# Attention in steps of four heads on the array's quarters, with MLP units in the last eight steps

## The chip, the cores and the metric

One core of a Trainium2 chip runs the kernel. The metric is the device time in microseconds of one execution; of the kernel before there are three runs. Times inside the kernel come from one profiled execution of it.

## The reference

```python
def _attn_ref(q, k, v, cap):            # (4, 12, 448, 64) each
    scale = 1.0 / np.sqrt(q.shape[-1])
    scores = scale * np.matmul(q, k.transpose(0, 1, 3, 2))
    scores = cap * np.tanh(scores / cap)
    scores = scores - np.max(scores, axis=-1, keepdims=True)
    attn = np.exp(scores)
    attn = attn / (np.sum(attn, axis=-1, keepdims=True) + 1e-09)
    return np.matmul(attn, v).astype(np.float32)

def _moe_ref(x, w1, w2, w3, w_out):     # x (1792, 768), weights (768, 768)
    h = np.maximum(np.maximum(x @ w1, x @ w2), x @ w3)
    return (h @ w_out).astype(np.float32)
...
    x = np.ascontiguousarray(attn_out.transpose(0, 2, 1, 3)).reshape(B * S, H * D)
    return _moe_ref(x=x, **moe_kwargs)
```

The cap is 30, so the kernel takes its branch without the row maximum (the tanh bounds the scores; the maximum cancels but for the 1e-9, which is scaled instead).

## The kernel before

**Attention.** There are 24 pairs of heads, one step each. The 448 keys of a pair are three tiles of 128 for each head and a tail tile that holds the last 64 keys of both heads. `scores` (L127) multiplies the three tiles, the two heads on the upper and lower 64 rows of the array, into three double banks `qk`; `scores_tail` (L136) multiplies the tail on the whole array with a block-diagonal key tile `kb`. ScalarE turns each tile into tanh (`tanh`, L145) and later into exp (`expo`, L149) in the tile `e_t`. `values_tail` and `values` (L152, L159) multiply with the values, the two heads on the left and right 64 columns of the array, and `sums` (L179) multiplies the VectorE sum `s_t` of the exp tiles with ones. `normalize` (L186) takes the reciprocals between two 32x32 transposes and multiplies; `split_x` (L197) writes the result as two fp32r tiles, `xh` and what that leaves, `xl`. All of these products are f32 and show in the trace as two matmul records each.

**MLP.** 24 weight tiles (18 for w1, w2, w3, then 6 for w_out) meet 4 batches of 448 tokens: 96 units (`unit`, L258). A unit is 18 fp32r matmuls (6 chunks of 128 inputs, three of the four high and low products each) into one bank. ScalarE copies the first of three weights into `m`, VectorE takes the maximum with the others. When the 18th weight tile of a batch is done, `split_h` (L278) splits that batch's six tiles for the last layer, a ScalarE cast and a VectorE subtraction each. The weights come as float64 words and `conv` (L233) makes two fp32r tiles of each in four steps: a ScalarE piece (L241) and a VectorE piece, two more VectorE pieces (L246, L250), then the ScalarE cast with L253 and a VectorE subtraction.

**Order.** The order on every engine is written out by hand in `rest` (L284); each engine works through its own list and waits where an operand is not there. In a step the products of pair i come first (scores), then values and sums of pair i-1, then its normalization; ScalarE does the tanh of pair i and, after those, its exp. The conversion of the first two weight tiles lies in the last eight steps. Only the first two units of the MLP stand ahead of the last pair's values. Loads go through SP's queue, two steps ahead.

Of the kernel before, what the change touches and what calls it, by code (L numbers as in the profile page):

```python
# [28 lines left out]
AHEAD = 2  # L29
UNITS_AHEAD = 2  # L30

EARLY = NP - 8
# [3 lines left out]
def attn_max_mlp_kernel(ctx: ExitStack, tc: tile.TileContext, q, k, v, kt, vt, cap, wts, out):  # L36

# [31 lines left out]
    q_t = ring("q_t", 3, [128, S])  # L69
    k_t = ring("k_t", 3, [128, NT * 128])  # L70
    v_t = ring("v_t", 3, [128, NT, 2, D])
    kb = ring("kb", 2, [128, PB, 128])
    vb = ring("vb", 2, [128, PB, 128])
    e_t = ring("e_t", 2, [128, 2 * NT + 1, S])
    s_t = ring("s_t", 2, [128, 2, S])
    tt_t, rb_t, xf_t = (ring(n, 2, [128, S]) for n in ("tt_t", "rb_t", "xf_t"))
    r_t = ring("r_t", 2, [128, QB])
    xh = ring("xh", NP, [128, S], F32R)
    xl = ring("xl", NP, [128, S], F32R)
# [4 lines left out]
    wl = ring("wl", 3, [128, KC, 128], F32R)  # L84

    qk = ring("qk", 3, [128, 2, 512], pool=psum)
    bk = ring("bk", 2, [128, 512], pool=psum)


    spare = [t[:, i, :] for t in e_t for i in range(2 * NT + 1)]  # L90
    spare += [t[:, i, :] for t in s_t for i in range(2)] + [*tt_t, *rb_t, *xf_t]
    m_t = {(b, f): m_0[b] if f == 0 else spare[B * (f - 1) + b] for f in range(KC) for b in range(B)}
    o_t = [*q_t, *spare[B * (KC - 1):]]

    banks = [t[:, i, :] for i in range(2) for t in qk] + [*bk]
# [4 lines left out]
    def flat(t):  # L100
        return t.rearrange("p a b -> p (a b)")


    def load_batch(b):
        for src, dst in ((kt, kb[b % 2]), (vt, vb[b % 2])):
            for h in range(2):
                r = slice(64 * h, 64 * h + 64)
                nc.sync.dma_start(out=dst[r, :, r], in_=src[b][r])

    def load(p):  # L110
        nc.sync.dma_start(out=k_t[p % 3], in_=k[p])
        nc.sync.dma_start(out=q_t[p % 3], in_=q[p])
        if p == 0:
            load_batch(0)
        nc.sync.dma_start(out=v_t[p % 3], in_=v[p])
        if p % PB == PB - 2 and p + 2 < NP:
            load_batch(p // PB + 1)

    turn = [0]

    def bank():
        turn[0] += 1
        return bk[turn[0] % 2]

    ps_tail, ps_av = {}, {}

    def scores(p):  # L127
        kt_, qt_ = k_t[p % 3], q_t[p % 3]
        for j in range(NT):
            for h in range(2):  # L130
                r = slice(64 * h, 64 * h + 64)
# [4 lines left out]
    def scores_tail(p):  # L136
        ps_tail[p] = bank()
        nc.tensor.matmul(ps_tail[p][:, 0:S], kb[p // PB % 2][:, p % PB, :], q_t[p % 3], start=True, stop=True)  # L138

    def e_of(p, j):  # L140

        e = e_t[p % 2]
        return e[:, 2 * NT, :] if j == NT else e[:, 2 * j:2 * j + 2, :]

    def tanh(p, j):  # L145
        src = ps_tail[p][:, 0:S] if j == NT else qk[j][:, :, 0:S]
        nc.scalar.activation(out=e_of(p, j), in_=src, func=AF.Tanh, scale=sc_t)  # L147

    def expo(p, j):  # L149
        nc.scalar.activation(out=e_of(p, j), in_=e_of(p, j), func=AF.Exp, scale=acap)  # L150

    def values_tail(p):  # L152
        ps_av[p] = bank()
        nc.tensor.matmul(  # L154
            ps_av[p][:, 0:S], vb[p // PB % 2][:, p % PB, :], e_of(p, NT), start=True, stop=False,
            skip_group_check=True,
        )

    def values(p):  # L159
        for j in range(NT):  # L160
            for h in range(2):
                nc.tensor.matmul(  # L162
                    ps_av[p][64 * h:64 * h + 64, 0:S], v_t[p % 3][:, j, h, :], e_of(p, j)[:, h, :],
                    start=False, stop=(j == NT - 1), skip_group_check=True,
                )

    def add_two(p):
        tt(nc.vector, flat(s_t[p % 2]), flat(e_of(p, 0)), flat(e_of(p, 1)), ALU.add)

    def add_rest(p):  # L170
        s = s_t[p % 2]
        for h in range(2):
            r = slice(64 * h, 64 * h + 64)
            tt(nc.vector, s[r, h, :], s[r, h, :], e_of(p, NT)[r], ALU.add)
        tt(nc.vector, flat(s), flat(s), flat(e_of(p, 2)), ALU.add)

    ps_sum = {}

    def sums(p):  # L179
        ps_sum[p] = bank()  # L180
        for h in range(2):
            nc.tensor.matmul(  # L182
                ps_sum[p][64 * h:64 * h + 64, 0:S], ones, s_t[p % 2][:, h, :], start=True, stop=True
            )

    def normalize(p, eps):  # L186

        t, r, rb, xf = tt_t[p % 2], r_t[p % 2], rb_t[p % 2], xf_t[p % 2]
        nc.vector.transpose(out=t, in_=ps_sum[p][:, 0:S])  # L189
        nc.vector.tensor_scalar_add(r, t.rearrange("p (a b) -> p a b", b=32)[:, :, 0], eps)  # L190
        nc.vector.reciprocal(r, r)
        nc.vector.transpose(  # L192
            out=rb.rearrange("p (a b) -> p a b", b=32), in_=r.unsqueeze(2).to_broadcast([128, QB, 32])
        )
        tt(nc.vector, xf, ps_av[p][:, 0:S], rb, ALU.mult)

    def split_x(p):  # L197
        xf = xf_t[p % 2]
        nc.vector.tensor_copy(out=xh[p], in_=xf)
        tt(nc.vector, xl[p], xf, xh[p].bitcast(F32), ALU.subtract)  # L200

    def rowmax(p):

        for h in range(2):
            rows = slice(64 * h, 64 * h + 64)
            tail = e_of(p, NT)[rows]
            parts = [e_of(p, j)[:, h, :] for j in range(NT)]
            mx, st, mb = g_mx, g_st, g_mb
            tt(nc.vector, mx, parts[0], parts[1], ALU.max)
            tt(nc.vector, mx, mx, parts[2], ALU.max)  # L210
            tt(nc.vector, mx[rows], mx[rows], tail, ALU.max)
            nc.vector.transpose(out=st, in_=mx)
            nc.vector.tensor_reduce(out=g_um, in_=st.rearrange("p (a b) -> p a b", b=32), op=ALU.max, axis=AX.X)
            for i in range(4):
                nc.vector.tensor_copy(out=g_um4[:, i, :], in_=g_um[32 * i:32 * i + 32])
            nc.vector.tensor_reduce(out=g_umr, in_=g_um4.rearrange("p i b -> p b i"), op=ALU.max, axis=AX.X)
            for i in range(4):
                nc.vector.tensor_copy(out=g_umb[32 * i:32 * i + 32], in_=g_umr)
            nc.vector.transpose(
                out=mb.rearrange("p (a b) -> p a b", b=32), in_=g_umb.unsqueeze(2).to_broadcast([128, QB, 32])  # L220
            )
            for t, r in [(t, slice(0, 128)) for t in parts] + [(tail, rows)]:
                tt(nc.vector, t, t, mb[r], ALU.subtract)

    g_mx, g_st, g_mb = m_0[0], m_0[1], m_0[2]
    g_um, g_umb = tl("g_um", [128, QB]), tl("g_umb", [128, QB])
    g_um4, g_umr = tl("g_um4", [32, 4, QB]), tl("g_umr", [32, QB])

# [4 lines left out]
    def conv(n, step):  # L233

# [10 lines left out]
        elif step == 1:  # L245
            nc.vector.scalar_tensor_tensor(  # L246
                out=w, in0=top, scalar=-0x80000000, in1=w, op0=ALU.bitwise_and, op1=ALU.bitwise_or
            )
        elif step == 2:
            nc.vector.scalar_tensor_tensor(  # L250
                out=w, in0=low, scalar=29, in1=w, op0=ALU.logical_shift_right, op1=ALU.bitwise_or
            )
            nc.scalar.copy(out=h, in_=d)  # L253
        else:
            tt(nc.vector, l, d, h.bitcast(F32), ALU.subtract)


    def unit(n, b, g):  # L258

        ps = banks[g % 8][:, 0:S]  # L260
        for kc in range(KC):
            w_h, w_l, a_h, a_l = wh[n % 3][:, kc, :], wl[n % 3][:, kc, :], xh[PB * b + kc], xl[PB * b + kc]
            nc.tensor.matmul(ps, w_h, a_h, start=(kc == 0), stop=False)  # L263
            nc.tensor.matmul(ps, w_h, a_l, start=False, stop=False)  # L264
            nc.tensor.matmul(ps, w_l, a_h, start=False, stop=(kc == KC - 1))  # L265
        if n >= 3 * KC:
            o = o_t[g % len(o_t)]
# [10 lines left out]
    def split_h(b, f):  # L278

        i = PB * b + f  # L280
        nc.scalar.copy(out=xh[i], in_=m_t[b, f])
        tt(nc.vector, xl[i], m_t[b, f], xh[i].bitcast(F32), ALU.subtract)

    def rest(general):  # L284
# [3 lines left out]
        def turn_of(n, b):  # L288
# [5 lines left out]
            if n == 3 * KC - 1:  # L294
                for f in range(KC):
                    split_h(b, f)
# [120 lines left out]
```

## Time and profile before

| | us |
|---|---|
| median of three runs | 554.19 |
| the three runs | 553.18, 554.19, 597.67 |
| span of the profiled execution | 551.0 |
| TensorE busy in it | 532.9 |
| ScalarE busy | 237.2 |
| VectorE busy | 280.4 |

The span is from the first to the last instruction of the profiled execution; the device time holds some microseconds around it. Busy times of the engines overlap. A matmul record is longer than the distance to the next one, since matmuls are pipelined, so TensorE's pace is read from start times, not from lengths.

### The profile page before, as it was taken

The numbers are of one execution on the slowest core, as the hardware profiler recorded it, in microseconds if no ns is written. First come the engines' busy times: TensorE is split into PE (matmuls) and PEld (weight loads), VectorE is DVE, ScalarE is ACT, GpSimd is POOL, SyncE is SP. The second block draws the span as 40 slices with busy tenths as digits, with TensorE's granted clock in tenths as the row PEclk, the third lists the DMA queues.
The fourth block names the chain that finished last, engine by engine and source line by source line (L and its number), as shares of the span: only waits on it lengthen the run. The fifth ranks groups of instructions, "written<-read, shape, count | busy, mean of one in ns | idle before, by whom it ended". The sixth has DMA issues, their size and how long they took to land.

```text
span 551.0 us, 6252 instructions
## 1 busy us (share of the span) xinstructions
PE 532.9 (97%) x2505; PEld 395.2 (72%) x2505; DVE 280.4 (51%) x438; ACT 237.2 (43%) x315; POOL 4.4 (1%) x15
## 2 busy tenths in 40 slices
PE   8999999999979799999999999999999999999997
PEld 4333333333323279999999999999999999999996
DVE  1888888889969783341432342333233269312200
ACT  6988889889778641112112103102102155222211
POOL 3000000000000000000000000000000000000000
PEclk9999999999999999999999999999999999999999
DMA  6232243433313101111111111102013010333112
GB/s 195 73 112 73 90 119 108 170 95 90 92 46 116 34 26 57 58 57 58 57 58 57 58 57 58 42 28 103 0 58 115 1 57 22 120 125 124 66 53 73
DMA packets 23748, 41.38 MB, mean 75 GB/s; under 512 B 8352, under 2 KB 20640, under 8 KB 23712
## 3 DMA queue, kind: packets, MB, share of 16 engines
q1 hardware_dynamic: 23680, 40.90, 22.9%
q8 instruction: 22, 0.36, 0.3%
q14 instruction: 14, 0.11, 0.1%
q0 software_dynamic: 32, 0.00, 0.0%
HBM read 35.39 MB, written 5.51 MB: 74 GB/s over the span
## 4 chain that ended last, share of the span: by engine, by line
PE 82%; DVE 14%; ACT 2%; issue 1%; DVEq 0%; ACTq 0%
PE qk L263 16%; PE qk L265 16%; PE qk L264 16%; PE bk L162 8%; PE bk L265 5%; PE bk L264 5%; PE bk L263 5%; PE bk L138 3%; DVE s_t L98 3%; PE bk L182 3%; PE bk L154 3%; DVE tt_t L189 3%; DVE rb_t L192 2%; DVE xf_t L98 2%; ACT e_t L147 1%
## 5 line engine op out<-in xcount | busy, mean ns | idle before, releaser
L263 PE MATMUL qk<-xh,wh 128*128 128x448 f32 x432 | 158.2, 366 | 0.0
L264 PE MATMUL qk<-xl,wh 128*128 128x448 f32 x432 | 157.9, 366 | 0.0
L265 PE MATMUL qk<-xh,wl 128*128 128x448 f32 x432 | 157.9, 366 | 0.0
L263 PEld LDWEIGHTS qk<-xh,wh 128*128 128x128 f32 x432 | 81.3, 188 | 7.7 <-issue 0.7
L265 PEld LDWEIGHTS qk<-xh,wl 128*128 128x128 f32 x432 | 81.3, 188 | 6.3
L264 PEld LDWEIGHTS qk<-xl,wh 128*128 128x128 f32 x432 | 81.3, 188 | 6.2
L253 ACT CAST wh<-cw 128x768 fp32r<-128x768 f32 x24 | 20.0, 835 | 147.7 <-DVE cw L250 147.7
L150 ACT ACTIVATE e_t<-e_t,acap 128x448 f32<-128x448 f32 (+1 forms) x96 | 83.2, 955 | 0.0
L147 ACT ACTIVATE e_t<-qk,sc_t 128x896 f32<-128x896 f32 x72 | 67.1, 1008 | 1.5 <-PE qk L132 1.5
L132 PE MATMUL qk<-q_t,k_t 64*128 64x448 f32 x288 | 61.2, 557 | 0.7 <-ACT e_t L147 0.7
L162 PE MATMUL bk<-e_t,v_t 128*64 128x448 f32 x288 | 59.4, 548 | 0.0
L98 DVE TENSOR_TENSOR s_t<-s_t,e_t 64x448 f32<-64x448 f32 (+1 forms) x72 | 56.0, 777 | 4.2 <-DVE s_t L98 0.5
L263 PE MATMUL bk<-xh,wh 128*128 128x448 f32 x144 | 52.7, 366 | 0.0
L264 PE MATMUL bk<-xl,wh 128*128 128x448 f32 x144 | 52.6, 366 | 0.0
L265 PE MATMUL bk<-xh,wl 128*128 128x448 f32 x144 | 52.6, 366 | 0.0
L132 PEld LDWEIGHTS qk<-q_t,k_t 64*128 64x128 f32 x288 | 26.0, 188 | 35.3 <-ACT e_t L147 17.5
L162 PEld LDWEIGHTS bk<-e_t,v_t 128*64 128x64 f32 x288 | 18.5, 136 | 37.9 <-issue 18.7
L98 DVE TENSOR_TENSOR e_t<-e_t,qk 128x448 f32<-128x448 f32 x22 | 13.7, 622 | 62.2 <-PE qk L265 62.2
L98 DVE TENSOR_TENSOR wl<-cw,wh 128x768 fp32r<-128x768 f32 x24 | 22.9, 955 | 35.7 <-ACT wh L253 35.7
L242 DVE TENSOR_SCALAR cw<-cw 128x768 int32<-128x768 int32 x24 | 13.3, 555 | 40.7 <-ACT cw L241 40.7
L98 DVE TENSOR_TENSOR s_t<-e_t 128x896 f32<-128x896 f32 x24 | 26.0, 1082 | 9.9 <-ACT e_t L150 9.9
L138 PE MATMUL bk<-q_t,kb 128*128 128x448 f32 x48 | 24.5, 592 | 6.0 <-DVE xf_t L98 6.0
(66 smaller groups left out, 395.4 us busy)
## 6 DMA issues: line engine op xcount, KB each, us to landing
wd<-in_wts_dram SPq DMA_DIRECT2D x24, 768.0 KB, 4.3
q_t<-in_q_dram SPq DMA_DIRECT2D x24, 224.0 KB, 3.2
k_t<-in_k_dram SPq DMA_DIRECT2D x24, 192.0 KB, 2.6
v_t<-in_v_dram SPq DMA_DIRECT2D x24, 192.0 KB, 2.4
out_dram<-q_t SPq DMA_DIRECT2D x10, 224.0 KB, 1.9
out_dram<-rb_t SPq DMA_DIRECT2D x8, 224.0 KB, 1.9
out_dram<-xf_t SPq DMA_DIRECT2D x6, 224.0 KB, 1.9
kb<-in_kt_dram SPq DMA_DIRECT2D x8, 96.0 KB, 3.1
```

Of the source, the lines that this page charges most:

```text
L98: eng.tensor_tensor(out=out, in0=in0, in1=in1, op=op)
L132: nc.tensor.matmul(qk[j][:, h, 0:S], kt_[r, 128 * j:128 * j + 128], qt_[r, :], start=True, stop=True)
L138: nc.tensor.matmul(ps_tail[p][:, 0:S], kb[p // PB % 2][:, p % PB, :], q_t[p % 3], start=True, stop=True)
L147: nc.scalar.activation(out=e_of(p, j), in_=src, func=AF.Tanh, scale=sc_t)
L150: nc.scalar.activation(out=e_of(p, j), in_=e_of(p, j), func=AF.Exp, scale=acap)
L154: nc.tensor.matmul(ps_av[p][:, 0:S], vb[p // PB % 2][:, p % PB, :], e_of(p, NT), start=True, stop=False, skip_group_check=True,)
L162: nc.tensor.matmul(ps_av[p][64 * h:64 * h + 64, 0:S], v_t[p % 3][:, j, h, :], e_of(p, j)[:, h, :], start=False, stop=(j == NT - 1), skip_g ...
L182: nc.tensor.matmul(ps_sum[p][64 * h:64 * h + 64, 0:S], ones, s_t[p % 2][:, h, :], start=True, stop=True)
L253: nc.scalar.copy(out=h, in_=d)
L263: nc.tensor.matmul(ps, w_h, a_h, start=(kc == 0), stop=False)
L264: nc.tensor.matmul(ps, w_h, a_l, start=False, stop=False)
L265: nc.tensor.matmul(ps, w_l, a_h, start=False, stop=(kc == KC - 1))
```

## The change

The heads go in 12 steps of four. A step's 448 keys are seven tiles of 64 for every head, so the tail tiles `kb` and `vb` and their loads are gone. Every attention product is four matmuls of 64 rows by 64 columns, one on each quarter of the array: `scores` writes a slot `qk` (two double banks, used in turn), `values` and `sums` write `av` and `sm` (one double bank each). A tile of tanh or exp is 128x896 for four heads, seven of each in a step. The tanh of a tile and the exp of the tile before alternate. VectorE adds the tiles one by one; in the steps of `BY_PE` the last tile is added by a second product in `sums` instead. `normalize` and `split_x` work on 896 columns.

In each of the steps 4 to 11 a unit of the MLP (`FILL`) runs on TensorE between value tile 6 of the step before and score tile 5, into a bank of `sm`; 88 units are left behind the attention. The pieces of `conv` (now five) lie in the steps given by `CONV`, ahead of the step's last exp. Behind the attention come the unit (2, 2) and two units of the last batch, held open at their last two chunks, and then the rest in order. `split_h` for all batches and tiles stands behind the last unit of the 18th weight tile, all batches of a tile before the next tile. The inputs are laid out for this on the host.

```diff
+FILL = {4 + i: (i % 3, i // 3) for i in range(8)}
+FILLED = [(2, 2)]
+BY_PE = (0, 1, 2, 3, 11)
+CONV = {0: [(0, k) for k in range(5)], 1: [(1, 0), (1, 1)], 2: [(1, 2), (1, 3), (1, 4)],
+        4: [(2, 0), (2, 1)], 5: [(2, 2), (2, 3), (2, 4)], 9: [(3, 0)], 10: [(3, 1)], 11: [(3, 2)]}
...
+    def scores(t, j):
+        ps = slot(t, j)
+        for R in range(2):
+            for s in range(2):
                 nc.tensor.matmul(
-                    qk[j][:, h, 0:S], kt_[r, 128 * j:128 * j + 128], qt_[r, :], start=True, stop=True
+                    ps[rows(s), R, 0:S], k_t[t % 2][rows(R), j, s, :], q_t[t % 2][rows(R), s, :],
+                    start=True, stop=True, skip_group_check=True,
                 )
...
+    def values(t, j):
+        for s in range(2):
+            for R in range(2):
                 nc.tensor.matmul(
+                    av[rows(R), s, 0:S], v_t[t % 2][rows(s), j, R, :], e_of(t, j)[rows(s), R, :],
+                    start=(j == 0), stop=(j == NJ - 1), skip_group_check=True,
                 )
...
+    def sums(t, by_pe):
+        parts = [s_t[t % 2]] + ([e_of(t, NJ - 1)] if by_pe else [])
...
+    def step(t, eps):
+        last = t - 1
+        if t:
+            sums(last, last in BY_PE)
+            recip(last, eps)
+            values(last, 3)
+        if t < NG:
+            tanh(t, 1)
+            expo(t, 0)
+            scores(t, 3)
+        if t:
+            values(last, 4)
+            values(last, 5)
+        if t < NG:
+            tanh(t, 2)
+            expo(t, 1)
+            add(t, 1)
+            scores(t, 4)
+        if t:
+            values(last, 6)
+            normalize(last)
+        if t < NG:
+            tanh(t, 3)
+            expo(t, 2)
+            add(t, 2)
+        if t:
+            split_x(last)
+        if 0 < t < NG - 1:
+            load_qk(t + 1)
+            load_v(t + 1)
+        if t == NG:
+            return
+        fill = FILL.get(t)
+        if fill:
+            products(*fill, sm[:, 0, 0:S], range(KC))
+        tanh(t, 4)
+        expo(t, 3)
+        if fill:
+            expo(t, 4)
+            empty(*fill, sm[:, 0, 0:S])
+        add(t, 3)
+        scores(t, 5)
+        values(t, 0)
+        tanh(t, 5)
+        if not fill:
+            expo(t, 4)
+        add(t, 4)
+        scores(t, 6)
+        values(t, 1)
+        if t + 1 < NG:
+            scores(t + 1, 0)
+        values(t, 2)
+        if fill:
+            expo(t, 5)
+            tanh(t, 6)
+        else:
+            tanh(t, 6)
+            expo(t, 5)
+        add(t, 5)
+        if t + 1 < NG:
+            scores(t + 1, 1)
+        for n, i in CONV.get(t, []):
+            conv(n, i)
+        expo(t, 6)
+        if t not in BY_PE:
+            add(t, 6)
+        if t + 1 < NG:
+            tanh(t + 1, 0)
+            scores(t + 1, 2)
...
+                if n == 3 * KC - 1 and b == B - 1:
+                    for f in range(KC):
+                        for bb in range(B):
+                            split_h(bb, f)
```

## Rows read from the trace of the kernel before

**Rows 1.** Stretches: length, busy us and instructions of each engine, granted clock, DMA share.

```profile
100.98:108.61 7.63, 7.38 (x34) 2.82 (x32) 6.65 (x11) 6.66 (x10) 0.00 (x0) 1.00 0.55 186
181.89:192.42 10.53, 7.61 (x34) 2.73 (x33) 7.83 (x13) 5.19 (x8) 0.00 (x0) 1.00 0.10 27
300.00:400.00 100.00, 100.00 (x495) 92.83 (x494) 33.19 (x46) 15.10 (x23) 0.00 (x0) 1.00 0.14 48
```

**Rows 2.** The page: span, granted clock in 40 slices, one group (busy, mean ns).

```profile
span 551.0 us, 6252 instructions
...
PEclk9999999999999999999999999999999999999999
...
L242 DVE TENSOR_SCALAR cw<-cw 128x768 int32<-128x768 int32 x24 | 13.3, 555 | 40.7 <-ACT cw L241 40.7
```

**Rows 3.** Timeline of one attention step: start, us, engine, line, operation, tiles, count.

```profile
100.13 0.92 PE L182 MATMUL bk<-s_t,ones 128*64 128x448 f32 x4
...
100.98 2.53 PE L132 MATMUL qk<-q_t,k_t 64*128 64x448 f32 x12
...
105.35 2.79 ACT L147 ACTIVATE e_t<-qk,sc_t 128x896 f32<-128x896 f32 x3
```

**Rows 4.** Groups by line and shape, 60 to 180 us: busy us, mean ns, idle before.

```profile
L147 ACT ACTIVATE e_t<-qk,sc_t 128x896 f32<-128x896 f32 x47 | 43.8, 1009 | 0.0
L150 ACT ACTIVATE e_t<-e_t,acap 128x896 f32<-128x896 f32 x45 | 43.6, 1048 | 0.0
...
L98 DVE TENSOR_TENSOR s_t<-s_t,e_t 128x896 f32<-128x896 f32 x16 | 17.5, 1093 | 1.7
...
L162 PEld LDWEIGHTS bk<-e_t,v_t 128*64 128x64 f32 x186 | 12.0, 136 | 24.4 <-ACT e_t L147 12.0 <-issue 11.8 <-ACT e_t L150 0.7
...
L189 DVE STREAM_TRANSPOSE tt_t<-bk 128x448 f32<-128x448 f32 x15 | 9.7, 648 | 9.4 <-PE bk L182 9.4
...
L98 DVE TENSOR_TENSOR xl<-xf_t,xh 128x448 fp32r<-128x448 f32 x15 | 9.4, 625 | 0.5
...
L199 DVE CAST xh<-xf_t 128x448 fp32r<-128x448 f32 x15 | 5.8, 386 | 0.0
...
L190 DVE TENSOR_SCALAR r_t<-tt_t,eps_f 128x14 f32<-128x14 f32 x15 | 3.5, 235 | 0.5
L241 ACT ACTIVATE cw<-wd 128x768 f32<-128x768 f32 x2 | 1.8, 918 | 0.0
```

**Rows 5.** Timeline of TensorE's weight loads ahead of one sum product.

```profile
16.09 0.23 PEld L182 LDWEIGHTS bk<-s_t,ones 128*64 128x64 f32 x4 [0.75 <-issue]
```

**Rows 6.** Timeline where attention meets the conversion and the first MLP units.

```profile
181.85 2.91 ACT L150 ACTIVATE e_t<-e_t,acap 128x896 f32<-128x896 f32 x3
...
189.11 0.95 DVE L250 SCALAR_TENSOR_TENSOR cw<-wd,cw 128x768 int32<-128x768 int32 x1
190.10 0.83 ACT L253 CAST wh<-cw 128x768 fp32r<-128x768 f32 x1 [5.34 <-DVE cw L250]
...
191.52 0.97 PE L182 MATMUL bk<-s_t,ones 128*64 128x448 f32 x4 [2.55 <-ACT e_t L147]
...
203.83 0.47 PE L263 MATMUL qk<-xh,wh 128*128 128x448 f32 x1
...
204.14 0.36 PE L264 MATMUL qk<-xl,wh 128*128 128x448 f32 x1
```

**Rows 7.** Timeline: the first tanh and the last matmul.

```profile
6.40 1.01 ACT L147 ACTIVATE e_t<-qk,sc_t 128x896 f32<-128x896 f32 x1 [1.48 <-PE qk L132]
...
546.64 0.37 PE L265 MATMUL bk<-xh,wl 128*128 128x448 f32 x1
```

**Rows 8.** Timeline of the splits of one batch: ScalarE's casts, VectorE's subtractions.

```profile
450.14 2.01 ACT L281 CAST xh<-e_t 128x448 fp32r<-128x448 f32 x4
...
454.70 2.22 DVE L98 TENSOR_TENSOR xl<-e_t,xh 128x448 fp32r<-128x448 f32 x4
```

**Rows 9.** The page's DMA issues: tile, queue, count, KB each, us to landing.

```profile
wd<-in_wts_dram SPq DMA_DIRECT2D x24, 768.0 KB, 4.3
```

More of the change, by code (lines that the diff above doesn't have):

```diff
@@ L84, in attn_max_mlp_kernel @@
     wl = ring("wl", 3, [128, KC, 128], F32R)
[L86 to L95, printed above, removed]
+    g_um, g_umb = tl("g_um", [128, 2 * QB]), tl("g_umb", [128, 2 * QB])
@@ new lines, in attn_max_mlp_kernel, with flat, quarters @@
+    g_um4 = tl("g_um4", [32, 4, 2 * QB])
+    qk = ring("qk", 2, [128, 2, 512], pool=psum)
+    sm = tl("sm", [128, 2, 512], pool=psum)
+    av = tl("av", [128, 2, 512], pool=psum)
+    halves = [t[:, i, :] for t in e_t for i in range(2)]
+    m_t = {(b, f): m_0[b] if f == 0 else halves[B * (f - 1) + b] for f in range(KC) for b in range(B)}
+    def flat(t):
+        return t.rearrange("p a b -> p (a b)")
+    def quarters(t):
+        return t.rearrange("p a b c -> p (a b c)")
+    o_t = [t[:, i, :] for i in range(2) for t in (*q_t, *s_t, *x_t)]
@@ L97, in tt @@
+    banks = [t[:, i, :] for a, b in ((qk[0], qk[1]), (sm, av)) for i in range(2) for t in (a, b)]
     def tt(eng, out, in0, in1, op):
         eng.tensor_tensor(out=out, in0=in0, in1=in1, op=op)
[L100 to L131, printed above, removed]
+    def rows(i):
+        return slice(64 * i, 64 * i + 64)
+    def load_qk(t):
+        nc.sync.dma_start(out=quarters(k_t[t % 2]), in_=k[t])
+        nc.sync.dma_start(out=flat(q_t[t % 2]), in_=q[t])
+    def load_v(t):
+        nc.sync.dma_start(out=quarters(v_t[t % 2]), in_=v[t])
@@ L140, in e_of @@
[L140 to L157, printed above, removed]
@@ L177, in attn_max_mlp_kernel @@
[L177 to L190, printed above, removed]
+                    av[rows(R), s, 0:S], v_t[t % 2][rows(s), j, R, :], e_of(t, j)[rows(s), R, :],
@@ new lines, in values, with add @@
+                    start=(j == 0), stop=(j == NJ - 1), skip_group_check=True,
+                )
+    def add(t, j):
+        s = flat(s_t[t % 2])
+        tt(nc.vector, s, flat(e_of(t, 0)) if j == 1 else s, flat(e_of(t, j)), ALU.add)
+    def sums(t, by_pe):
+        parts = [s_t[t % 2]] + ([e_of(t, NJ - 1)] if by_pe else [])
+        for i, part in enumerate(parts):
+            for s in range(2):
+                for R in range(2):
+                    nc.tensor.matmul(
+                        sm[rows(R), s, 0:S], ones[rows(s), :], part[rows(s), R, :],
+                        start=(i == 0), stop=(i == len(parts) - 1), skip_group_check=True,
+                    )
@@ L194, in normalize @@
         )
[L195 to L223, printed above, removed]
@@ L252, in conv @@
             )
+        elif step == 3:
             nc.scalar.copy(out=h, in_=d)
@@ L255, in conv, with products @@
             tt(nc.vector, l, d, h.bitcast(F32), ALU.subtract)
[L258 to L262, printed above, removed]
+    def products(n, b, ps, kcs):
+        for kc in kcs:
+            w_h, w_l, a_h, a_l = wh[n % 3][:, kc, :], wl[n % 3][:, kc, :], xh[b][:, kc, :], xl[b][:, kc, :]
             nc.tensor.matmul(ps, w_h, a_h, start=(kc == 0), stop=False)
@@ L278, in split_h @@
     def split_h(b, f):
[L280 to L284, printed above, removed]
-        eps = eps_g if general else eps_f
+        h, l = xh[b][:, f, :], xl[b][:, f, :]
+        nc.scalar.copy(out=h, in_=m_t[b, f])
+        tt(nc.vector, l, m_t[b, f], h.bitcast(F32), ALU.subtract)
+    def step(t, eps):
[67 more added lines that the diff above has]
+            scores(t + 1, 2)
@@ new lines, in general_attention @@
+    def general_attention():
+        for t in range(NG):
+            if t:
+                load_qk(t)
+                load_v(t)
+                for j in range(2):
+                    scores(t, j)
+                tanh(t, 0)
+                scores(t, 2)
+            for j in range(1, NJ):
+                tanh(t, j)
+                if j + 2 < NJ:
+                    scores(t, j + 2)
+            rowmax(t)
+            for j in range(NJ):
+                expo(t, j)
+                values(t, j)
+                if j:
+                    add(t, j)
+            sums(t, False)
+            recip(t, eps_g)
+            normalize(t)
+            split_x(t)
@@ new lines, in bank, with whole @@
+            return banks[(g - 1) % 8][:, 0:S]
+        def whole(n, b):
+            ps = bank()
+            products(n, b, ps, range(KC))
+            empty(n, b, ps)
+            done.add((n, b))
+        fast = bool(done)
+        if fast:
+            for n, b in FILLED:
+                whole(n, b)
+            held = []
+            for n in range(2):
+                held.append(bank())
+                products(n, B - 1, held[n], range(KC - 2))
+            for n in range(2):
+                products(n, B - 1, held[n], range(KC - 2, KC))
+                empty(n, B - 1, held[n])
+                done.add((n, B - 1))
+                if n == 0:
+                    for i in (3, 4):
+                        conv(3, i)
```

229 lines of the change are left out of this document (119 added, 110 removed).

## The prediction

> **What bounds the kernel now.** I read three stretches in order of time. The table of stretches comes first [rows 1]: in one attention step, 100.98 to 108.61, TensorE is busy nearly all the time and ScalarE for 6.66 of 7.63 us; in the MLP (300 to 400) TensorE is never idle and 495 matmuls take 100 us, 0.202 us each, so a unit of 18 takes 3.65 us. The page's clock line shows full clock throughout [rows 2]. The MLP is therefore TensorE time and nothing else: 94 of its 96 units run from 203.83 to 546.84 [rows 6, 7], and the change alters no matmul in them. What can move is the attention before 203.83, the number of units left after it, and any hole between units.
>
> The timeline of one attention step shows what TensorE's time there is made of [rows 3]. An f32 product is two records (12 for the six score products of a pair of heads). Each record lasts about 0.55 us, but four sum records take 0.92 us together: two start times 0.375 apart, two records at each. So two halves of the array run side by side, and a product costs 0.75 us for a pair. The loop issues both passes of one half before those of the other, so the second half starts ahead of a pass issued earlier. A pair costs three score, one tail score, one tail value, three value and one sum product: nine times 0.75, 6.75 of 7.63 us. Four heads cost 15.26 us.
>
> **The change, by parts.** Quarters: four heads then cost 7 score groups, 7 value groups and 1 sum group (2 in steps 0 to 3 and 11), if the four quarters of a group run side by side as the halves do. No row shows quarters. Row halves run together (the scores), and so do column halves (the sums), each with its own data stream [rows 3]. The weight loads of halves run together under the matmuls, 0.136 us each for 64 columns [rows 4]. Issue is no limit: four loads, with three matmuls between them, begin within 0.23 - 0.14 = 0.09 us [rows 5], so the 16 instructions of a group need under 0.25 us. Bounds: 0.75 us a group (all four together) and 1.5 (two at a time). I take 0.75, as both kinds of halves run at that pace.
>
> The Trainium skill ("TensorE: Matmul & The Clock Gate", Part 3: Packing small matmuls) says that matmuls start strictly in program order, and that a weight load overlaps running matmuls only in another row group. The trace disagrees with both: column halves share all rows and their loads still hide, and halves pass an earlier second pass. By the first rule a group would be 1.5 us and the total some 660, by the second about 1.0 and 582; by the rows it is 0.75.
>
> Other unit costs. Three tanh in 2.79 us, one of them 1.009: they start 0.89 apart [rows 3, 4]. Three exp in 2.91: 0.93 apart [rows 6]. VectorE: an add of 128x896 1.09, of 128x448 0.625, so 448 more elements cost 0.47; a transpose of 896 is then 0.65 + 0.47 = 1.12, the cast 0.39 to 0.85 (I take 0.62), the small ones 0.24 [rows 4].
>
> ScalarE's own sum for a step of four heads is 7 x 0.89 + 7 x 0.93 = 12.7. VectorE's is two transposes, two small ones, the product, the split and five adds: 11.2, or 12.3 with the sixth add.
>
> A plain step (1 to 3), in us from the start of the last exp of the step before. The next step's first tanh starts at 0.93 and ends at 1.94; it frees the bank for score tile 2, which TensorE runs from 2.0 to 2.75. Both sum groups end at 4.25, value tile 3 and score tile 3 at 5.75. ScalarE, through two tanh and two exp, could take tile 3 at 5.46 but sees it at 5.96; tile 4 likewise at 8.2. From there it runs unhindered: tanh 6 at 11.8, the last exp at 13.7. VectorE begins its reciprocals at 4.5 and ends the fifth add at 16.2, 2.5 into the next step, just ahead of the sums at 2.75. So 13.7 us against 15.26.
>
> A fill step (4 to 11): one sum group, so TensorE is at 8.0 after value tile 6. Then the unit: 0.2 for the change of array shape (0.1 idle, and the next start 0.31 instead of 0.20 later [rows 6]), 3.65, and about as much back (I take 0.15): 12.0. Score tile 5 is seen at 12.95, where ScalarE has waited since 10.2. Tanh 5, exp 5, tanh 6, exp 6 now follow each other with the full 1.01 and 1.05 in between: the last exp starts at 16.05. TensorE's own sum is 11.25 + 3.65 + 0.35 = 15.25, so this step is its chain with 0.8 us of waiting.
>
> The weight conversions lie before the last exp. A ScalarE piece takes 0.92 [rows 4], a VectorE one 0.55 [rows 2] or 0.95, the ScalarE cast 0.83, and ScalarE waits for VectorE before the cast; before, that wait was 5.34 us [rows 6]. Behind the cast in ScalarE's queue stand the last exp and the next step's first tanh, and TensorE's score tile 2 and sums wait for those. Step 0 has the whole conversion: first tanh at 6.4 [rows 7], thirteen ScalarE steps to 11.8, first piece, then VectorE's add and three pieces to 15.6, cast, last exp at 16.4. Step 1: 13.7 + 0.85 = 14.5. Step 2: VectorE's fifth add ends at 16.2, its piece at 17.2, cast, exp at 18.05. Step 4 has two sum groups and a ScalarE piece: 17.5. Step 5: add 16.2, piece 17.2, cast, exp at 18.05. Step 9: 16.75. Steps 6, 7, 8, 10, 11: 16.05 each; the copies and maxima of the units lie in ScalarE's or VectorE's waits.
>
> Sum: first tanh 6.4, step 0 16.4, steps 1 to 3 46.2, steps 4 to 11 17.5 + 18.05 + 16.75 + 80.25 = 132.5; that is 201.6 for the last exp of step 11. Its end, one sum group and four value groups with the shape change: 5.05, so the MLP begins at 206.6. The first unit and two held ones (8.5 us, no need of the last heads) cover the last normalization and split (about 6). 88 units x 3.65 = 321.2.
>
> A hole is added. Before, each batch's six tiles were split right after its 18th unit, under the next units. Now all 24 splits stand behind the last of these units, tile by tile over the batches. The next unit needs batch 0's sixth tile, the 21st of the 24. ScalarE starts casts 0.48 apart and VectorE the subtractions 0.535 apart [rows 8]; VectorE also has a maximum and a conversion piece first. It ends the 21st some 1.7 + 21 x 0.535 = 13 us after the unit; the next unit then ends at 13.5 instead of 3.65. Price 9.8 us, at least about 8 if VectorE's head start is nothing, at most 13 if the first product waits for all. What else waits is three more units of batches 1 to 3, whose tiles come 0.5 us apart: no further loss.
>
> The end is as before, 551.0 - 546.84 = 4.15 us behind the last matmul [rows 7]. Loads: a step fetches three tiles of 448 KB and at times 768 KB of weights; 768 KB land in 4.3 us [rows 9], and each tile is asked for half a step or more ahead. SP's queue holds each value load until the old values are used, 8 us into a step, with the next key and query load behind it; both still land a step ahead. I cost it at nothing; if it were uncovered, about 2 us a step.
>
> 206.6 + 321.2 + 9.8 + 4.15 = 541.8 against a span of 551.0 [rows 2]. The runs' median, 554.19, lies 3.2 above that span; I leave this unchanged: 545. Some 2% is about what a measurement of this kernel tells from no change: 543.1 to 565.3 is "same".
>
> **Rivals.** (A) Forecast: groups at 0.75 us, the step held by the chain above, a hole of 8 to 13. Own range 536 to 556 (fill steps of 15.3 to 17). Chance 0.62.
>
> (B) The quarters don't all run at once. At 1.5 us a group a fill step takes 16.05 + 11.25 = 27.3 and a plain one 24: 90 and 26 us more, about 660. It decides earlier: the 120 groups of fill steps make 20 us at 0.17 more each, so from 0.92 us a group the kernel is over 2% slower. For it: no row shows a quarter. Against it: both kinds of halves keep 0.375. The weight loads left uncovered (two of 0.136) are the mild form, about 1.02 a group: 545 + 120 x 0.27 and a little in plain steps, some 582. Together 0.12, of which 0.04 is the mild form, since loads are covered in every row.
>
> (C) The waits that I put in series hide behind each other: fill steps at TensorE's 15.25, conversions free. 122 + 41 instead of 178.7 for steps 1 to 11: 15.5 less, 529.5. For it: ScalarE has 12.7 us of work only. Against it: tanh 5 can't start before the unit is through. 0.16.
>
> (D) The clock falls where TensorE now idles: in step 0, and in the hole, where it works about 0.6 of every 2.1 us. No row shows the lower level; 18 matmuls at half the clock would cost a unit up to 3.65 more. Two or three units, and waits of 0.05 to 0.1 that I left out: 8 to 14 us, 553 to 559. Before, an idle stretch of 2.55 us ahead of the sums at 191.52 left the clock at 1.00 [rows 1, 6]. 0.10.
>
> **Numbers.** Faster (under 543.1): C and 0.42 of A, 0.42. Slower (over 565.3): B and a rest of D, 0.13. Same: 0.45. The range takes C and D in: 528 to 562; B lies outside.
>
> **What would show it.** Score and value records of the new kernel: eight per group, starting in two clusters 0.375 apart (A), four clusters (B). Steps by the distance of last exps: 13.7, 16.05, and 18 in steps 2 and 5. ScalarE's idle time ahead of tanh 5 of some 2.8 us in fill steps, with the unit as cause. A hole of about 10 us at the 73rd unit of the 96, waiting for VectorE's splits; full clock behind it, or not (D). MLP start near 206 with 88 units to go. The prediction is wrong if a group is not near 0.75 us, or if fill steps miss 15.3 to 17.

## The result and the profile after

| | before | after |
|---|---|---|
| first comparison, median of four runs each, us | 559.01 | 559.06 |
| ratio after to before, with its interval | | 1.0103 [1.0055, 1.0151] |
| second comparison (19 runs and 10), median, us | 553.49 | 554.77 |
| ratio after to before, with its interval | | 1.0026 [0.9997, 1.0055] |
| span of the profiled execution, us | 551.0 | 557.2 |

(The medians are over all runs; the ratios leave disturbed runs out.) The change moves the time by less than this kernel's measurement can tell from nothing. The forecast was 545, a gain of 1.7%; 559 lies inside its range, and the expected gain did not come.

The page of the changed kernel: its span, the granted clock in 40 slices, and two groups (busy, mean ns, idle before).

```profile
span 557.2 us, 7444 instructions
...
PEclk9899899989999999999999999999999986999999
...
L117 PE MATMUL qk<-q_t,k_t 64*64 64x448 f32 x672 | 81.8, 560 | 25.1 <-ACT e_t L123 24.7
...
L123 ACT ACTIVATE e_t<-qk,sc_t 128x896 f32<-128x896 f32 x84 | 83.0, 1002 | 23.2 <-PE qk L117 22.1
```

Where the line of before was 9 in all slices [rows 2], three slices now stand lower in the attention and two around 450 us. TensorE waits 25 us ahead of score products, nearly all of it for ScalarE's tanh, which has to read a bank before new scores go into it.

The table of stretches of the changed kernel, in the columns of [rows 1] (the clock is the third number from the end): three places of the attention, fill step 8, the MLP, and the place where the last layer begins.

```profile
22.70:29.50 6.80, 2.90 (x16) 1.05 (x20) 2.07 (x3) 5.55 (x7) 0.00 (x0) 0.50 0.00 0
60.30:63.60 3.30, 3.09 (x20) 1.09 (x24) 0.00 (x0) 3.23 (x5) 0.00 (x0) 0.50 0.00 0
111.50:114.80 3.30, 3.30 (x20) 1.14 (x20) 0.20 (x2) 3.28 (x4) 0.00 (x0) 0.50 0.00 0
143.30:159.30 16.00, 15.44 (x142) 7.70 (x138) 12.33 (x15) 13.20 (x14) 0.00 (x0) 1.00 0.39 136
300.00:400.00 100.00, 100.00 (x486) 90.83 (x485) 32.73 (x46) 15.52 (x22) 0.00 (x0) 1.00 0.17 56
456.20:469.80 13.60, 10.83 (x26) 7.62 (x26) 12.35 (x22) 6.80 (x14) 0.00 (x0) 0.50 0.05 17
```

Four of the six stand at 0.50, the lower of the clock's two levels (1.2 GHz). The MLP stretch is at full clock with TensorE busy throughout, and yet it holds 486 matmuls where before had 495 [rows 1]. By their start times they lie 0.2067 us apart in place of 0.2027.

What TensorE did before the clock fell, from its timeline (start, us, line, operation, and the idle time just before): the ends of steps 0, 2 and 5.

```profile
26.61 1.77 PE L117 MATMUL qk<-q_t,k_t 64*64 64x448 f32 x8 [6.23 <-ACT e_t L123]
...
60.51 1.02 PE L117 MATMUL qk<-q_t,k_t 64*64 64x448 f32 x4 [4.88 <-ACT e_t L123]
...
111.33 0.99 PE L117 MATMUL qk<-q_t,k_t 64*64 64x448 f32 x4 [2.39 <-ACT e_t L123]
```

It was idle for 6.23, 4.88 and 2.39 us, waiting for ScalarE's first tanh of the next step, which stands behind the conversion's cast in ScalarE's queue. The first group behind the wait is drawn out: its eight records last 1.77 us, where those of the quick groups below last 0.93.

The same timeline where the last layer begins.

```profile
451.54 0.37 PE L218 MATMUL qk<-xh,wh 128*128 128x448 f32 x1
453.82 0.47 PE L219 MATMUL qk<-xl,wh 128*128 128x448 f32 x1 [1.91 <-DVE xl L95]
...
455.96 0.58 PE L219 MATMUL qk<-xl,wh 128*128 128x448 f32 x1 [1.27 <-DVE xl L95]
...
465.06 0.57 PE L220 MATMUL qk<-xh,wl 128*128 128x448 f32 x1
465.43 0.57 PE L218 MATMUL qk<-xh,wh 128*128 128x448 f32 x1
...
469.88 0.37 PE L218 MATMUL qk<-xh,wh 128*128 128x448 f32 x1
470.09 0.37 PE L219 MATMUL qk<-xl,wh 128*128 128x448 f32 x1
```

This is the hole: each chunk waits for its `xl`. The clock falls inside it, and from 465.06 matmuls come 0.37 us apart instead of 0.21 until 469.88, when no wait is left.

**The account.** From the forecast's span of 541.8 to 557.2, in us:

| part | forecast | measured | difference |
|---|---|---|---|
| start to last exp of step 0 | 22.8 | 24.6 | +1.8 |
| steps 1 to 11 | 178.7 | 183.7 | +5.0 |
| last exp to MLP | 5.05 | 5.0 | 0 |
| pace of 88 units (88 x 18 matmuls, 0.004 us slower each) | 321.2 | 327.4 | +6.2 |
| hole | 9.8 | 12.2 | +2.4 |
| end | 4.15 | 4.3 | +0.1 |

The hole is what remains of the MLP's 339.6 us (213.36 to 552.95) behind 327.4. The experiments below take these terms one by one.

### The profile page after: what moved, and what is told of

The parts are those of the page before. It is cut to its first block, busy times and chain, and to the rows that moved or that the text cites. A ratio compares the mean times of both kernels' runs of the same rounds, so it can differ in the third digit from the quotient of the medians.

```text
span 557.2 us, 7444 instructions
## 1 busy us (share of the span) xinstructions
PE 518.9 (93%) x3217; PEld 383.8 (69%) x3217; DVE 257.9 (46%) x325; ACT 235.2 (42%) x291; POOL 1.1 (0%) x7
## 4 chain that ended last, share of the span: by engine, by line
PE 80%; ACT 12%; DVE 5%; issue 1%; ACTq 0%; DVEq 0%
PE qk L219 10%; PE qk L218 10%; PE qk L220 10%; PE sm L218 7%; PE qk L117 7%; PE sm L220 7%; PE sm L219 7%; ACT e_t L123 6%; PE av L131 6%; PE av L218 5%; PE av L220 5%; ACT e_t L126 5%; PE av L219 5%; PE sm L145 3%; DVE xl L95 2%; DVE s_t L95 1%
## 5 line engine op out<-in xcount | busy, mean ns | idle before, releaser
L219 PE MATMUL qk<-xl,wh 128*128 128x448 f32 x264 | 99.8, 378 | 6.0 <-DVE xl L95 6.0
L117 PE MATMUL qk<-q_t,k_t 64*64 64x448 f32 x672 | 81.8, 560 | 25.1 <-ACT e_t L123 24.7
L220 PE MATMUL qk<-xh,wl 128*128 128x448 f32 x264 | 98.9, 375 | 0.0
L218 PE MATMUL qk<-xh,wh 128*128 128x448 f32 x264 | 98.9, 375 | 0.0
L126 ACT ACTIVATE e_t<-e_t,acap 128x896 f32<-128x896 f32 x84 | 86.3, 1038 | 0.4
L131 PE MATMUL av<-e_t,v_t 64*64 64x448 f32 x672 | 75.9, 538 | 1.4 <-DVE x_t L95 1.4
L218 PE MATMUL sm<-xh,wh 128*128 128x448 f32 x180 | 67.0, 372 | 0.0
L220 PE MATMUL sm<-xh,wl 128*128 128x448 f32 x180 | 66.2, 368 | 0.0
L219 PE MATMUL sm<-xl,wh 128*128 128x448 f32 x180 | 66.1, 367 | 0.0
L95 DVE TENSOR_TENSOR s_t<-s_t,e_t 128x896 f32<-128x896 f32 x55 | 59.9, 1088 | 11.5 <-ACT e_t L126 10.0
```

The source lines that it names most:

```text
L95: eng.tensor_tensor(out=out, in0=in0, in1=in1, op=op)
L117: nc.tensor.matmul(ps[rows(s), R, 0:S], k_t[t % 2][rows(R), j, s, :], q_t[t % 2][rows(R), s, :], start=True, stop=True, skip_group_check=True,
L126: nc.scalar.activation(out=e_of(t, j), in_=e_of(t, j), func=AF.Exp, scale=acap)
L131: nc.tensor.matmul(av[rows(R), s, 0:S], v_t[t % 2][rows(s), j, R, :], e_of(t, j)[rows(s), R, :], start=(j == 0), stop=(j == NJ - 1), skip_ ...
```

## The experiments

Theories, after the comparison of the traces: (1) the slower MLP pace belongs to the execution, not to the change; (2) the splits that stand in one lump behind the 18th weight tile cost about 12 us; (3) the conversion steps that stand together ahead of a step's last exp cost their own wait and, by TensorE's idling, the clock behind it. Rivals: that the change itself slows the MLP, that the splits cost the same wherever they stand, that attention loses its time to the fill units.

**The kernel before, profiled once more.** No edit.

> The kernel before, once more, with a profile. In the changed kernel's profile the MLP matmuls start 0.2067 us apart, in the profile of before 0.2027. If that pace belongs to the kernel, this profile shows 0.2027 and a time near 553. If it belongs to the execution or the chip, it may show 0.2067 and a time near 560 (1728 matmuls x 0.004 = 7 us more).

561.39 us, span 559.5. Two stretches of this execution, columns as above, and the wait ahead of the first.

```profile
192.70:196.10 3.40, 3.40 (x10) 3.02 (x11) 2.40 (x5) 3.40 (x5) 0.00 (x0) 0.50 0.33 136
300.00:400.00 100.00, 100.00 (x486) 90.81 (x485) 31.91 (x45) 15.28 (x23) 0.00 (x0) 1.00 0.14 48
```

```profile
191.65 0.97 PE L182 MATMUL bk<-s_t,ones 128*64 128x448 f32 x4 [2.55 <-ACT e_t L147]
```

The unchanged kernel ran its MLP at 486 matmuls in 100 us, the pace of after; in its first profile it had 495 [rows 1]. So the slower pace needs no change of the kernel, and 94 units x 18 x 0.004 = 6.8 us hang on it. (It doesn't belong to the whole execution either: the two units ahead of the last values ran at 0.2027 here. The last experiment comes back to this.) The other 1.7 of the 8.5 us between its two spans are the 3.4 us at half the clock, which here followed an idle time of 2.55 us; the same idle time had left the clock alone in the first profile [rows 1, 6].

**The splits put back behind each batch's own unit.**

```diff
-                if n == 3 * KC - 1 and b == B - 1:
+                if n == 3 * KC - 1:
                     for f in range(KC):
-                        for bb in range(B):
-                            split_h(bb, f)
+                        split_h(b, f)
```

> Each batch's splits right behind its 18th unit, as before; all else as changed. If the hole at the 73rd unit is the 24 splits in a row, and the clock fell because of it, the hole goes and the clock stays at 1.00 there: 451.5 to 465.4 becomes one unit (3.7), 10.1 us less, and some 13 matmuls at the low clock (0.37 instead of 0.21) give back 2.2 more: about 12 us less, 547. Rival: the clock falls there for another reason: 10 less and a low stretch stays.

540.08, 540.96, 548.07 and 548.42 us, ratio to before 0.9814 [0.9742, 0.9885]. The profiled run, 548.42, went at the slow pace (485 in 300 to 400), so its span of 546.6 stands against the 557.2 of after at the same pace: 10.6 less, with an attention that took 1.4 longer. The edit is worth 12.0 of the hole's 12.2. At the faster pace it comes out alike: 540.08 and 540.96 stand 12 below the shortest runs of after (552.5, below). The stretch in which the last layer begins:

```profile
440.00:460.00 20.00, 20.00 (x99) 18.16 (x98) 16.68 (x30) 13.00 (x26) 0.00 (x0) 1.00 0.01 1
```

Nearly all of the 24 casts and subtractions lie in it (the first two casts start just ahead of it, the last two subtractions just behind), TensorE is not idle, and the clock stays full.

**The conversion spread thinner over the early steps.**

```diff
-CONV = {0: [(0, k) for k in range(5)], 1: [(1, 0), (1, 1)], 2: [(1, 2), (1, 3), (1, 4)],
-        4: [(2, 0), (2, 1)], 5: [(2, 2), (2, 3), (2, 4)], 9: [(3, 0)], 10: [(3, 1)], 11: [(3, 2)]}
+CONV = {0: [(0, 0), (0, 1), (0, 2)], 1: [(0, 3), (0, 4), (1, 0), (1, 1)], 2: [(1, 2)],
+        3: [(1, 3), (1, 4), (2, 0), (2, 1)], 4: [(2, 2)], 5: [(2, 3), (2, 4)],
+        9: [(3, 0)], 10: [(3, 1)], 11: [(3, 2)]}
...
-                if t in (3, 8):
-                    conv_load(2 if t == 3 else 3)
+                if t in (1, 8):
+                    conv_load(2 if t == 1 else 3)
```

> The conversion pieces spread so that ScalarE never waits for VectorE's piece in the same step (the cast comes a step later); all else as changed. Theory: the waits of steps 0, 2 and 5 (3.3, 4.1, 1.9 us) and the lower clock right behind each (steps 1, 3 and 6 longer by 1.6 to 1.7) have one cause: steps 0 to 6 of 118.8 us in the changed kernel become about 107, time about 547, no low clock before 200 us. Rival: the low clock comes from the quarters or from few matmuls in plain steps: the waits go (some 7 us) but the low stretches and their 5 us stay, 552.

548.23 us (seven runs, 543.23 to 551.91), ratio 0.9879 [0.9839, 0.9919]. From the first tanh to the end of step 6 it took 111.9 us instead of 118.8: 6.9 less, not the 12 of the theory. The waits for the cast are gone, but the clock still fell; TensorE's timeline and two stretches (lines of this kernel are one further down).

```profile
40.08 1.77 PE L118 MATMUL qk<-q_t,k_t 64*64 64x448 f32 x8 [2.40 <-ACT e_t L124]
...
55.55 0.98 PE L118 MATMUL qk<-q_t,k_t 64*64 64x448 f32 x8 [0.88 <-ACT e_t L124]
```

```profile
40.00:43.40 3.40, 3.32 (x20) 1.29 (x24) 1.23 (x2) 3.34 (x5) 0.00 (x0) 0.50 0.00 0
53.60:56.90 3.30, 2.42 (x28) 0.82 (x24) 3.05 (x3) 3.30 (x5) 0.00 (x0) 1.00 0.73 237
```

At the end of step 1 two ScalarE steps of the conversion still stand ahead of the tanh, TensorE waits 2.40 us without any wait for VectorE, and the clock halves. At the end of step 2, with a wait of 0.88, it stays. So theory (3) held for the waits only, and the saving is the rival's (some 7 us, with low stretches left). The clock also falls without a wait for the cast. Whether idling of any kind brings it down, or what the quarters do, this run leaves open; the zeros below decide it.

**No units in the attention.** `FILL` is empty; the eight units run with the others behind the attention.

```diff
-FILL = {4 + i: (i % 3, i // 3) for i in range(8)}
+FILL = {}
```

> No MLP units in the steps (96 units behind the attention); all else as changed. Theory: a fill step of 16.1 us becomes a plain one of 13.7, about 19 less in steps 4 to 11 together, and 8 units x 3.7 = 30 come back in the MLP: 10 to 11 us slower than the changed kernel, 570. Rival (steps held by TensorE's own sum): steps fall to 11.6, the units cost nothing net: 559 to 561. Where idle TensorE lets the clock fall, steps get longer and the time more than 570.

572.53 us (570.87 to 575.52), ratio 1.0337 [1.0312, 1.0362]. Some 18 us more than after, though the eight units themselves are 29 us of TensorE's time. Steps 4 to 11 took 121.5 us, against 134.4 with the units in the second profile of after (below), which went at the same pace; 19 less had been expected. TensorE now idles in nearly every step, and the clock fell in more places, one of them here, where waits of 1.70 and 1.10 us lie close together:

```profile
94.90:101.70 6.80, 5.87 (x32) 2.03 (x36) 4.64 (x6) 3.49 (x5) 0.00 (x0) 0.50 0.00 0
```

The rival that attention loses its time to the fill units falls: without them the kernel is 18 us slower.

**The changed kernel again, ten runs.** No edit.

> The changed kernel unchanged, for its spread. MLP matmuls run at one of two paces in an execution, 0.2027 or 0.2067 us, in both kernels. If that alone spreads the times, its runs fall into two groups about 6.5 us apart, 552.5 and 559; against runs of before at the faster pace (553.6) the first group is a ratio of about 0.998. Rival: the change itself brings the slower pace: all runs near 559.

554.77 us (552.47 to 561.24), ratio 1.0026 [0.9997, 1.0055]; the profiled run, 552.5, has a span of 550.4. Its MLP:

```profile
300.00:400.00 100.00, 100.00 (x495) 92.68 (x495) 33.18 (x46) 15.00 (x22) 0.00 (x0) 1.00 0.17 56
```

The changed kernel has both paces too, and the times fall into two groups: seven from 552.47 to 555.0 and three from 558.49 to 561.24. Pace alone does not spread them: within each group the lower mean clock goes with the longer time (552.5 at 0.974 and 554.8 at 0.967; 558.49 at 0.975 and 561.24 at 0.968), so how often the clock falls changes from run to run too. At equal pace the spans are 550.4 after against 551.0 before, and 557.2 against 559.5, of which 1.7 are the low stretch of that execution: in either pair the change itself is worth some 0.6 us, which the interval of the ratio can't tell from nothing. One question of the rival stays open: of 32 executions of before that were measured beside the experiments one took more than 556 us (563.24), of these ten of after three did. Whether the change makes the slower pace more frequent no run settles.

**TensorE kept busy at the ends of the early steps.** Products of zeros into a bank that the next sums overwrite, so the results are the same.

```diff
+KEEP = {0: 26, 1: 9, 2: 20, 3: 9, 5: 10}
...
+        for _ in range(KEEP.get(t, 0)):
+            nc.tensor.matmul(sm[:, 0, 0:S], wz[:, 0:128], wz, start=True, stop=True)
         if t + 1 < NG:
             tanh(t + 1, 0)
             scores(t + 1, 2)
```

> The changed kernel with matmuls of zeros added on TensorE where it waits at the ends of steps 0, 1, 2, 3 and 5 (26, 9, 20, 9, 10 of them), into a bank that is written anew next; the waits themselves stay. Theory: the clock falls because TensorE idles there. Then the granted clock stays at 1.00 behind steps 0 to 5, steps 1, 3 and 6 go from 16.1, 15.4, 17.8 to 14.5, 13.7, 16.1, and the time falls by 5 us at either pace (548 or 554). Rival: the clock falls for what the quarters do, whatever TensorE does between: the low stretches stay, and the time with them.

554.31 us (ten runs, 549.71 to 556.29), ratio 0.9995 [0.9963, 1.0027]. Three stretches that answer to the three low ones of after:

```profile
22.70:29.50 6.80, 6.04 (x47) 3.90 (x49) 2.41 (x4) 5.42 (x7) 0.00 (x0) 1.00 0.00 0
55.00:75.00 20.00, 18.91 (x165) 9.94 (x167) 13.45 (x15) 17.38 (x19) 0.00 (x0) 1.00 0.33 121
105.00:125.00 20.00, 19.86 (x176) 10.25 (x168) 15.31 (x17) 16.01 (x19) 0.00 (x0) 1.00 0.28 91
```

The waits for ScalarE are still there, only filled, and the clock stays full throughout the attention. Steps 1, 3 and 6, each behind a low stretch in after, went from 16.08, 15.37 and 17.78 us to 14.65, 13.86 and 16.09; the forecast, without a fall of the clock, had 14.5, 13.7 and 16.05. That shows the cause of 4.6 of the 5.0 us: idle TensorE, not the quarters. The other nine runs agree by their mean clock, 0.982 to 0.988 in all ten, against 0.967 to 0.975 in the ten of after. The MLP began at 210.18 instead of 213.36 and 213.8: 3.2 to 3.6 were won, as zeros that ran too long cost about 1.2 back (step 2: 18.11 instead of 17.83, step 4: 18.52 instead of 17.55). The two medians differ by only 0.5 all the same: the spread over paces is larger than the gain. The shortest runs differ by 2.8 (549.71 against 552.47).

**The splits, the spread conversion and an earlier load of the cap together.** The first tanh of after waits for it, in ScalarE's timeline:

```profile
7.35 0.20 ACT L400 ACTIVATE acap<-cap_t 128x1 f32<-128x1 f32 x1 [5.33 <-DMA cap_t<-in_cap_dram]
...
8.30 1.91 ACT L123 ACTIVATE e_t<-qk,sc_t 128x896 f32<-128x896 f32 x2 [0.51 <-DVE eps_f L408]
```

```diff
-        nc.gpsimd.dma_start(out=cap_t, in_=cap.partition_broadcast(128))
+        nc.sync.dma_start(out=cap_t, in_=cap.partition_broadcast(128))
```

(Here it stands at the head of SP's queue, ahead of the large loads; the other two edits are those above.)

> Splits behind each batch's 18th unit, conversions spread, and the cap's own transfer first on SP's queue instead of GpSimd's. Theory, each on its own account: 12 less, 8 less, and the first tanh at 6.7 instead of 8.3 (1.6 less), since ScalarE's first work waited 5.3 us for that transfer. Sum: 552.5 - 21.6 = 531 at the faster pace, 537 at the slower. If the gains overlap, 535 or more at the faster pace.

538.43 us (538.16 to 540.01), ratio 0.9732 [0.9709, 0.9756]; span 536.5 at the slow pace, 20.7 less than after at that pace, about the sum of 12.0, 7.2 (its span of 543.2 against 550.4) and 1.4. The same place:

```profile
3.59 0.20 ACT L400 ACTIVATE acap<-cap_t 128x1 f32<-128x1 f32 x1 [1.58 <-DMA cap_t<-in_cap_dram]
...
6.92 1.90 ACT L124 ACTIVATE e_t<-qk,sc_t 128x896 f32<-128x896 f32 x2 [2.89 <-PE qk L118]
```

The clock still fell three times, 3.4 us each, behind waits of 2.40 to 2.56 us.

**The same with fewer zeros:** `KEEP = {0: 9, 1: 9, 2: 9, 3: 12, 4: 4}`, no more than the 2.4 us waits take.

> The kernel with the three mended, and matmuls of zeros at the ends of steps 0 to 4 (9, 9, 9, 12, 4). Theory (idle TensorE lets the clock fall): no low stretch between 20 and 90 us, steps 1 to 4 shorter by 1.7 where one was: 3 to 5 less than with the three alone, 527 at the faster pace. Rival: nothing changes, or the zeros delay the steps by what they take.

532.34 us (528.7, 529.3, 535.37, 535.89: two paces), ratio 0.9596 [0.952, 0.9671]; span 533.5 at the slow pace, 3.0 less than without the zeros. This version beats both kernels. Its page and two stretches:

```profile
PEclk9999999999999999999999999999999999999999
```

```profile
20.00:50.00 30.00, 28.11 (x272) 11.79 (x270) 24.99 (x30) 28.43 (x32) 0.00 (x0) 1.00 0.30 105
50.00:100.00 50.00, 49.54 (x441) 24.82 (x437) 39.47 (x46) 42.06 (x47) 0.00 (x0) 1.00 0.25 84
```

**The MLP's stream broken before every eighth unit,** by one short product of zeros, to see whether the pace belongs to the execution or to a running stream.

```diff
+            if g % 8 == 0:
+                nc.tensor.matmul(ps[:, 0:64], wz[:, 0:128], wz[:, 0:64], start=True, stop=True)
```

> The kernel with three mended and zeros, with one short matmul (64 columns of zeros) ahead of every eighth unit of the MLP. Which of the two paces, 0.2027 or 0.2067, an execution gets is open. Theory: it is taken where an unbroken stream of matmuls begins and kept until it is broken; then the stretches of eight units between breaks have either pace, both in one execution, and times lie between the two groups of the kernel without breaks (528.9 and 535.6) plus some 2 us for the breaks. Rival: an execution has one pace throughout (chip, clock or placement), and the stretches all agree.

530.51 and 532.28 us, ratio 0.9589 [0.9527, 0.965], not to be told from the version without breaks. Two stretches of 21 us, before and behind the first break at 227.6:

```profile
206.00:227.00 21.00, 21.00 (x104) 19.06 (x103) 8.04 (x11) 4.68 (x7) 0.00 (x0) 1.00 0.17 54
232.00:253.00 21.00, 21.00 (x105) 19.47 (x104) 6.66 (x10) 2.49 (x4) 0.00 (x0) 1.00 0.10 38
```

Within one execution the matmuls came 206.6 ns apart before the first break, and 202.6 behind it and behind the ten later ones. So the rival, one pace throughout an execution, falls. The other profiles bear the theory out. In all eleven, a stream of MLP matmuls keeps the pace at which it starts until TensorE does something else or waits; none changes on the way. Streams of one execution differ: in the first profile of after, the fill unit of step 8 ran at the faster pace and that of step 11 at the slower. From the first to the last line of each pair are 15 matmuls, 3.04 and 3.10 us, 202.7 and 206.7 ns each:

```profile
151.95 0.36 PE L220 MATMUL sm<-xh,wl 128*128 128x448 f32 x1
...
154.99 0.36 PE L220 MATMUL sm<-xh,wl 128*128 128x448 f32 x1
...
200.89 0.37 PE L220 MATMUL sm<-xh,wl 128*128 128x448 f32 x1
...
203.99 0.37 PE L220 MATMUL sm<-xh,wl 128*128 128x448 f32 x1
```

In the profile of the changed kernel with zeros at the ends of steps the MLP ran at 206.7 ahead of the hole and at 202.7 behind it. What picks the pace where a stream starts stays open.

The clock fell once in this execution, in step 0, where TensorE had no wait over 0.84 us; without the breaks, with the same attention, it had not fallen.

```profile
12.36 1.38 PE L119 MATMUL qk<-q_t,k_t 64*64 64x448 f32 x8 [0.84 <-ACT e_t L125]
```

```profile
12.90:16.20 3.30, 3.30 (x24) 1.17 (x20) 2.18 (x2) 3.30 (x5) 0.00 (x0) 0.50 0.30 125
```

## Why the prediction was right and wrong

**Right: the quarters.** Groups of the changed kernel in fill step 8, from TensorE's timeline:

```profile
156.08 0.93 PE L131 MATMUL av<-e_t,v_t 64*64 64x448 f32 x8
156.83 0.93 PE L117 MATMUL qk<-q_t,k_t 64*64 64x448 f32 x8
157.58 0.93 PE L131 MATMUL av<-e_t,v_t 64*64 64x448 f32 x8
```

Eight records every 0.75 us, in two clusters 0.375 apart, the four of a cluster within 0.02 us. Rival (B) falls in both its forms. The Trainium skill's rule behind its mild form ("TensorE: Matmul & The Clock Gate", Part 3: Packing small matmuls: weight loads overlap running matmuls only in another row group) does not agree with these rows: uncovered loads would not leave 0.75. Its other rule, that matmuls start in program order, would by the prediction have made 1.5 us of a group. That holds only if both passes of a quarter are issued before the next quarter's, an order that the trace does not show; what it shows is that the price of 1.5 was wrong.

**Right: the chain of a fill step.** Steps 7, 8, 10 and 11 took 16.07 to 16.14 us against 16.05, step 9 took 16.74 against 16.75. ScalarE's timeline in step 8 has the wait that was to show it, 2.63 us ahead of tanh 5 (the forecast said some 2.8):

```profile
156.33 1.01 ACT L123 ACTIVATE e_t<-qk,sc_t 128x896 f32<-128x896 f32 x1 [2.63 <-PE qk L117]
157.37 1.04 ACT L126 ACTIVATE e_t<-e_t,acap 128x896 f32<-128x896 f32 x1
158.32 0.99 ACT L123 ACTIVATE e_t<-qk,sc_t 128x896 f32<-128x896 f32 x1
159.34 1.04 ACT L126 ACTIVATE e_t<-e_t,acap 128x896 f32<-128x896 f32 x1
```

Steps 2, 4 and 5 took 17.83, 17.55 and 17.9 (18.05, 17.5, 18.05). The waits add up as the forecast had them, so rival (C) falls; loads cost nothing. (By its own terms VectorE's sum for a step is 11.0, not 11.2, and the last exp of step 11 comes at 201.5, not 201.6; nothing hangs on either.)

**Right in kind: the hole,** at the 73rd unit, for VectorE's splits; 12.2 instead of 9.8. About 2.2 of the difference are 13 matmuls at 0.373 in place of 0.207, so without the clock the term was sound.

**Wrong: the clock.** The step that failed is the last sentence of (D): "an idle stretch of 2.55 us ahead of the sums at 191.52 left the clock at 1.00". That row was one execution; in another the same wait was followed by half the clock. The change makes longer waits (6.23 and 4.88 us) and two of 2.2 to 2.4, and the clock fell behind three of these four and in the hole: 5.0 us in steps 1, 3 and 6, each of which begins in a low stretch, and some 2.2 in the hole. (D) had this mechanism at 8 to 14 us and a chance of 0.10; it is what happened, at 7 us. The forecast had itself worked out the waits that cause it, as conversion steps ahead of the last exp, and priced only their length.

**Wrong: the MLP's pace.** "The change alters no matmul in them" was right, but the 3.65 us of a unit, read from one execution [rows 1], was taken for a property of the kernel. Each stream of such matmuls goes at 0.2027 or at 0.2067, in both kernels, and over 88 units that is 6.3 us: most of the 9.2 us by which the span was to shrink. The step that failed here is the term 88 x 3.65 = 321.2; in the first profile it measured 327.4. The change does not make the slower pace, since before has it too; whether it makes it more frequent is open.

**Mis-sized: the two ends.** The first tanh was left at 6.40 [rows 7], but it came at 8.30: ScalarE's first work on the cap starts 2.9 us later than before (7.35 instead of 4.48), while the larger loads of the new step run. That these loads delay it is argued: the run that cured it changed the queue and the order at once. And the 3.2 us between span and median, left unchanged, came of comparing one execution's span with the median of three: where both are of one run they lie 2.0 apart (559.23 and 557.2).

**Where the gain went.** At the pace that the forecast used, the span is 550.4: 8.6 above the forecast's 541.8, and some 0.6 below before. What quarters and fill units gain was given back: 12 in the hole, some 7 in waits and clock around the conversion, 1.4 at the start, and 3 more in the clock of the steps. Of these the forecast had priced the hole at 9.8 and the waits by their length, but not the clock. That the time came out the same as before, and inside the range, was luck: two terms that the sum left out, the clock and the pace, used up the gain. The version with all four mended is 23.7 us shorter than after at the same pace (533.5 against 557.2).

**Open:** what picks the pace at the start of a stream of matmuls, whether the change shifts the odds, and why a wait of about 2.2 to 2.5 us is followed by the low clock in some places and not in others. Single waits can't be the whole of it, as the fall behind waits of 0.84 us shows.

## What to carry to other kernels

Price a wait of TensorE twice: by its length, and by the work behind it at half the clock; a row in which the clock once survived such a wait is no proof. Work that one layer owes the next (splits, conversions) belongs under running matmuls as soon as each piece is ready, not in a lump at the seam. Before a pace per matmul is carried through hundreds of them, read it from several streams and several executions.

## What the runs showed of the hardware

- Streams of fp32r products (128x128 weights, 448 columns) run at 202.7 or 206.7 ns each at full granted clock. In eleven profiles each unbroken stream kept the pace at which it started, and most executions had streams of both.
- Behind single TensorE waits of 0.88 to 1.71 us at the ends of steps the clock stayed at 1.00 (after, and the spread conversion); behind waits of 2.20 to 2.57 it did both; behind 4.88 and 6.23 it was 0.50 each time. Two waits of 1.70 and 1.10 us close together also lie at a fall, and so do two of 0.84 in step 0 of the run with breaks.
- The low clock puts the same products 0.373 us apart instead of 0.207, and f32 groups of four quarters last 1.77 us instead of 0.93.
- Four 64x64 quarters start within 0.02 us of each other; four f32 products of 448 columns take 0.75 us.
- A small transfer on GpSimd's queue was waited for until 7.35 us while large loads ran from SP's queue, and until 3.59 us at the head of SP's queue.
